# Fused attention and MLP block: weight casts behind the kept sum in ten groups, and six single operations in other places

## The chip, the cores and the metric

The kernel runs on one core of a Trainium2 chip. The metric is device time in microseconds (us), the median of several runs. Engines are named as the profile names them: PE (matrix products; PEld its weight loads), ACT (ScalarE), DVE (VectorE), POOL (GpSimd) and SP (SyncE, which issues most DMAs). Each engine works through its own instructions strictly in the order in which the program wrote them; engines wait for one another through semaphores.

## The reference

```python
x = A_x                                   # (1, 2048, 576), float32
xn = layernorm(x)
# A: sliding, dilated attention, 32 heads of 18, window 8, dilation 2
q, k, v = split(xn @ wqkv)
A = softmax(mask(q . k[pos - 2 w]) * 18**-0.5) . v[pos - 2 w] @ wo
# B: spatial shift, then an MLP with 4608 hidden columns
y  = layernorm(xn)
h  = gelu(y @ w1); hs = shift(h) @ w2     # four quarters shifted by +1, -1, +2, -2 rows
x1 = xn + hs
B  = x1 + gelu(layernorm(x1) @ w3) @ w4
out = x + A + B
```

All arithmetic is float32. The kernel makes each float32 operand into a rounded high part and a low part (the rest) and multiplies high by high, high by low and low by high; so most operands are split by a cast on ACT (the high part) and a subtraction on DVE (the low part).

## The kernel before

The 2048 rows are 16 tiles of 128 rows, or 4 blocks of 512. The program is written out in one order by hand; the Python functions only record instructions, and the place of a call in the text is the instruction's place on its engine.

*First tiles.* For each row tile: statistics (`stats_x`, DVE, with one power on POOL), normalisation in place (`norm_x`, DVE), transposes on PE (`turn_x`, `turn_tail`), and `cast_x`, which splits the transposed tile: a cast on ACT (line 311) and a subtraction on DVE (line 312). `split_tail` does the same for weights, its subtraction here on POOL (line 260). `q_part` are the products for q, k and v. Then come the shift mixer and the second layer norm.

*The MLP, first part.* Six pairs of hidden tiles run plainly, as units (c, b) of a pair c and a block b. `up(u, c, b, i)` makes one hidden tile with 14 products (line 1136) in the order of the list `PAIRS`, which takes for each row chunk k: high by high, high by low, low by high. `x1n[b]` is the normalised block; planes 0 to 4 are high parts, 5 to 8 low parts, and `split_n` writes them piece by piece on ACT (917) and DVE (900). `down` then multiplies the hidden tile with w4 into an output tile (line 1172, 12 products).

*The MLP, groups.* The other 12 pairs run as 24 groups q, twelve for each half of the rows, each with seven products of sums of blocks instead of eight plain ones. A group has 15 steps: P1 to P7 (`product`, seven matmuls each, line 1436) and D0 to D7 (`down`, twelve matmuls each, line 1172, of the group before). Their order stands in the strings `ORDER` and `ORDERS`; from group 13 on it is P1 D0 P2 P6 D1 P5 D2 P7 D3 P4 D4 P3 D5 D6 D7. What other engines do is hung on steps by `at(step, function)` and is recorded right behind the step. The pieces that matter here:

- P1 begins the sum `ca` in a PSUM bank; ACT copies it into the bank of P2 (line 1641). P6 and P7 add to `ca`, and after each of them `keep` copies the sum to SBUF on ACT (line 1442); P4 adds to the same bank once more and so must wait until the copy behind P7 has read it. `z_add` (DVE, 1446) adds another product to a kept sum, and `gelu_z` (ACT, 1124 and 1125) makes the hidden tile of it.
- `split_a(n, steps)` makes the next group's weights `w3a`: steps 0 and 1 are two casts on ACT (lines 1274 and 1276) and a small accumulating DMA from POOL (1287); step 2 is a subtraction on DVE (1280). `combine` builds sums of weights on DVE (1269), and `split_s` makes `w3s` of these in the same three steps (1274, 1276 with the DMA of line 1296, 1280).
- A step D writes one of two PSUM tiles in turn (`ps0`, `ps1`). The result leaves through ACT into a staging tile and an accumulating DMA issued by POOL (1177 and 1178; the tile must be free, that is, an earlier DMA must have landed), through ACT (1180) or through DVE (1183). Some tiles are seeded: ACT copies the old sum into PSUM ahead of the step (1153). Two steps later the tile is used again, so a late departure holds that step.

`bg` hands out the attention's work on DVE in small pieces between the steps of groups up to 18. At group 12 the half changes, and operands are split anew (`split_op`).

*The end.* The last eight down tiles run after the groups, in the loop over `j`, while `split_x` splits the attention's output blocks (ACT lines 149, 150, 155; DVE lines 151, 156); its parts are 2 (the tail chunk), 3 (chunks 0 and 1) and 1 (chunks 2 and 3), and part 0 is 2 and 3 together. The products with wo follow (line 183) and the rows are stored.

Of the kernel before, what the change touches and what calls it, by code (L numbers as in the profile page):

```python
# [37 lines left out]
NWP = NF // 2 - NPL  # L38
# [3 lines left out]
PAIRS = []  # L42
# [15 lines left out]
def fused_block(ctx, tc, x, wqkv, wo, w1, w2, w3, w4, out):  # L58
# [86 lines left out]
    def split_x(xt, part=None, scr=None):  # L145
        raw = xt.bitcast(F32)
        if part in (None, 0, 2):
            r = xt[:, 9, :] if scr is None else scr.bitcast(F32R)
            act.copy(r[64:128], raw[64:128, 4, :])
            act.copy(xt[0:64, 4, :], raw[0:64, 4, :])  # L150
            dve.tensor_tensor(xt[64:128, 4, :], raw[64:128, 4, :], r[64:128].bitcast(F32),
                              op=ALU.subtract)
        for h in {None: (0, 1), 0: (0,), 1: (1,), 2: (), 3: (0,)}[part]:
            hi, lo = slice(2 * h, 2 * h + 2), slice(2 * h + 5, 2 * h + 7)
            act.copy(xt[:, hi, :], raw[:, lo, :])
            dve.tensor_tensor(xt[:, lo, :], raw[:, lo, :], raw[:, hi, :], op=ALU.subtract)
# [55 lines left out]
    def stats_x(t):  # L212
        stats(Y[:, t, :], 0, t)
# [36 lines left out]
    def hi_main(raw, b, o, k):  # L250
        act.copy(WB[b][:, o + k, 3:5, :], raw[:, k, 1:3, :])

    def lo_main(raw, b, o, k, eng=dve):
        eng.tensor_tensor(WB[b][:, o + k, 1:3, :], raw[:, k, 1:3, :],
                          WB[b][:, o + k, 3:5, :].bitcast(F32), op=ALU.subtract)
# [72 lines left out]
    def plain_x(t):  # L328
        return x_ops(("q", t // 4)), 2 * (t % 4)
# [7 lines left out]
    def cast_x(t, tail=False):  # L337
        (cast_tail if tail else cast_main)(*plain_x(t), 2, turns[t])
# [41 lines left out]
    def spill(stg, t, c0, n):  # L380
# [5 lines left out]
                   key=lambda s: (s[1] == 0, s[1] < 3, s[2] < 3))  # L386
# [57 lines left out]
    cast_x(0)  # L444
    hi_main(r0, 0, 0, 1)
    lo_main(r0, 0, 0, 1, pool)
    stats_x(2)
    cast_x(1)
    tails(1, act.copy)
    split_tail(r0, 0, 0, pool)  # L450
    pq = {t: psa.tile([128, 512], F32, name="p1", tag="a") for t in range(2)}
# [207 lines left out]
    for p in range(3, 8):  # L659
        n = p + 1  # L660
        plan = {k: () for k in range(23)}

        def at(k, f, *args):
            plan[k] += ((f,) + args,)
# [263 lines left out]
    for t in range(NT):  # L928
# [19 lines left out]
        if t in (4, 5):  # L948
            r0, c0, n = ((256, 128, 128), (HF + 256, 0, 256))[t - 4]
# [149 lines left out]
    def temp(t, n=512):  # L1099
        return Y[:, t, :n]  # L1100
# [31 lines left out]
    def up(u, c, b, i):  # L1132
        f = c * C + i
        ps = psa.tile([128, 512], F32, name="p1", tag="a")
        for n, (a, w) in enumerate(PAIRS):
            pe.matmul(ps, W3[f][:, w, :], x1n[b][:, a, :], start=n == 0, stop=n == len(PAIRS) - 1)  # L1136
        g = temp((7, 5)[i])
        h = hid[u, i] = gelu_ps((("c12", "c22"), ("c21", "c11"))[u % 2][i], ps, g)
        low_part(h, g)
# [321 lines left out]
    otile, xo = {}, {}  # L1461
# [29 lines left out]
    def o_turn(t):  # L1491
# [4 lines left out]
    ORDER = "P1 D0 P2 P6 D1 P5 D2 P7 D3 P4 D4 P3 D5 D6 D7"  # L1496
    ORDERS = {0: "P1 P2 D0 P6 P5 P7 D1 D2 P4 P3 D3",
              NWP - 1: "P1 D0 P2 P6 P5 P7 D1 P4 P3 D2 D3 D4 D5 D6 D7",
              NWP: "D0 D1 P1 D2 P2 P6 D3 P5 P7 D4 P4 P3 D5 D6 D7"}
    spent[0] = 0.0  # L1500
    for q in range(NQ):
        sb = q // NWP
# [29 lines left out]
        n = q + 1  # L1532
# [5 lines left out]
        if q == 0:  # L1538
            at("D0", split_op, 0, "T4")
            at("P6", split_op, 0, "B22")  # L1540
            at("P7", split_a, n, (0, 1))
            at("D1", gelu22)
            at("D1", split_a, n, (2,))
            at("D1", combine, n, 0, 2)
            at("D2", combine, n, 2, 4)
            at("P3", split_s, n, (0,))
            at("P3", gelu12)
            at("P3", low22)
            at("D3", low12)
            at("D3", split_s, n, (1, 2))  # L1550
            at("D3", load_pair, q + 2)
        elif q == NWP - 1:
            rtemps[:] = [2, 13]
            at("P1", load_w4, p, 1)
            for it, k in zip(("P1", "P2", "P6", "P5", "P7", "P4", "P3"),
                             ("B11", "B21", "T2", "T1", "T3", "T4", "B22")):
                at(it, get_op, 1, k)
            at("P4", split_w4, p)
            at("P3", split_op, 1, "B11", 0)
            at("D2", split_op, 1, "B11", 1)  # L1560
            at("D3", gelu22)
            at("D4", low22)
            at("D4", split_op, 1, "B21", 0)
            at("D5", gelu12)
            at("D5", split_op, 1, "B21", 1)
            at("D6", low12)
            at("D6", split_op, 1, "T2", 0)
            at("D7", split_op, 1, "T2", 1)
        elif q == NWP:
            rtemps[:] = [2]  # L1570
            at("D0", split_op, 1, "T1", 0)
            at("D1", split_op, 1, "T1", 1)
            at("P1", split_op, 1, "T3", 0)
            at("D2", split_op, 1, "T3", 1)
            at("P2", split_op, 1, "T4", 0)
            at("P6", split_op, 1, "T4", 1)
            at("D3", split_op, 1, "B22", 0)
            at("P5", split_op, 1, "B22", 1)
            at("P5", split_a, n, (0, 1))
            at("P7", split_a, n, (2,))  # L1580
            at("P7", combine, n, 0, 2)
            at("D4", combine, n, 2, 4)
            at("D4", gelu22)
            at("P4", low22)
            at("D5", gelu12)
            at("D5", split_s, n, (0,))
            at("D6", low12)
            at("D6", split_s, n, (1, 2))
            at("D7", load_pair, q + 2)
        elif z < -1:  # L1590
            at("P1", load_w4, p, 1)
            at("P5" if q < NWP else "D2", split_a, n, (0, 1))
            at("D2" if q < NWP else "P7", split_a, n, (2,))
            at("D3", combine, n)
            at("P4", gelu22)
            at("D4", split_w4, p, 0)
            at("D4", low22)
            at("D5", split_w4, p, 1)
            at("P3", split_s, n, (0, 1))
            at("D5", gelu12)  # L1600
            at("D5", split_s, n, (2,))
            at("D6", low12)
            if z < -2:
                at("D6", load_pair, q + 2 + (q == NWP - 2))
        else:
            at("D3", split_w4, p)
            at("P4", gelu22)
            at("D4", low22)
            at("D5", gelu12)
            at("D6", low12)  # L1610
            for k, it in enumerate(("P4", "D4", "P3", "P3", "D7")):
                at(it, split_wo, k)
# [89 lines left out]
    for j in range(8):  # L1702
        tiles[j]()
        if j == 0:
            low_part(h21, Z4)
            load_y((1, 2, 3, 5))
            EV[0] = (9, 11, 10, 15, 13)
        if j in (0, 2):
            split_x(xo[0], j // 2)
        if j == 6:  # L1710
            split_x(xo[1], 0)
        if j == 2:
            read_xo(2, xp_tile(3))
        if j == 5:
            load_y((7,))
            read_xo(3, ring_block(("o", 3)))
# [4 lines left out]
    for t in range(NT):  # L1721
        b, i = divmod(t, 4)
# [55 lines left out]
```

## Time and profile before

| what | us |
|---|---|
| median of 3 runs | 1268.59 (1267.49 to 1269.87) |
| the profiled execution, its own time | 1268.14 |
| its span from first to last instruction | 1266.4 |
| PE busy | 1254.4 |
| DVE busy | 933.0 |
| ACT busy | 761.6 |

The profile lists instructions with their start and duration in us from the span's start; in brackets stands how long the engine was idle just before, and what ended that. Rows with xN are N instructions of one kind in a row. Matmuls overlap a little: a step's modelled duration is longer than the distance from its start to the next step's start, so times lost on PE are read from distances between starts.

### The profile page before, as it was taken

To read this page: it belongs to the slowest core of one execution; us is meant where nothing else is said; L and a number is where in the kernel's file an instruction comes from. 1 tells how busy PE (TensorE), PEld (TensorE's weight loads), DVE (VectorE), ACT (ScalarE), POOL (GpSimd) and SP (SyncE) were. 2 spreads that over 40 slices of the span, in tenths; PEclk is the share of its full clock that TensorE was granted. 3 is DMA by queue.
4 is the path that set the end of the run, shared out by engine and by line. 5 is a ranking of instruction groups with operands and counts; after the bars stand their busy time and mean duration, and the time that the engine had idled before them with its cause. 6 is when DMAs were issued, how large, how long until landed. Compare 5 with 4: busy or idle time off the path is not lost.

```text
span 1266.4 us, 20999 instructions
## 1 busy us (share of the span) xinstructions
PE 1254.4 (99%) x7819; PEld 1156.8 (91%) x7819; DVE 933.0 (74%) x1207; ACT 761.6 (60%) x1271; POOL 266.9 (21%) x408
## 2 busy tenths in 40 slices
PE   8999999999999999999999999999999999999998
PEld 8999998899898999999889999998888899899998
DVE  7877646688558999997759998989889884464441
ACT  4455457526645545455867767776677776677620
POOL 2213200011222211212222232222122222222200
PEclk9999999999999999999999999999999999999999
DMA  7638994447888986769679898888968769899972
GB/s 220 157 85 199 229 197 146 149 130 198 200 230 180 222 158 147 159 135 245 124 175 192 194 200 190 189 166 206 249 111 183 141 116 194 185 213 223 263 245 84
DMA packets 208654, 228.92 MB, mean 181 GB/s; under 512 B 80920, under 2 KB 142328, under 8 KB 208424
## 3 DMA queue, kind: packets, MB, share of 16 engines
q1 hardware_dynamic: 175800, 160.79, 45.2%
q0 software_dynamic: 32752, 66.80, 32.6%
q8 instruction: 61, 1.00, 0.3%
q14 instruction: 41, 0.34, 0.1%
HBM read 127.71 MB, written 110.23 MB: 188 GB/s over the span
## 4 chain that ended last, share of the span: by engine, by line
PE 42%; issue 5%; DMA 2%; POOL 1%; ACT 1%; DVE 0%; POOLq 0%; ACTq 0%
PE ps L1172 20%; PE cc L1436 18%; PE ps L183 4%; DMA yd<-Y 1%; POOL yd L1178 1%; DMA w3s<-w3st 1%; PE p L1745 0%; DVE w3st L1269 0%; ACT Y L1177 0%; POOL w3s L1296 0%; ACT xt L1240 0%; ACT w3s L1274 0%; ACT cc L1641 0%; ACT Y L1442 0%; POOL w3a L1287 0%
## 5 line engine op out<-in xcount | busy, mean ns | idle before, releaser
L1172 PEld LDWEIGHTS ps<-w,c 128*128 128x128 f32 x3456 | 478.2, 189 | 15.3 <-ACT Y L1177 1.4
L1172 PE MATMUL ps<-w,c 128*128 128x288 f32 x3456 | 487.7, 296 | 1.1 <-ACT Y L1177 0.6
L1178 POOL DMA_DIRECT2D yd<-Y x154 | 138.0, 899 | 391.9 <-ACT Y L1177 333.0
L1130 DVE TENSOR_TENSOR c<-Y,c 128x512 fp32r<-128x512 f32 x144 | 98.8, 688 | 91.5 <-ACT Y L1119 87.9
L1177 ACT COPY Y<-ps 128x576 f32<-128x576 f32 x154 | 97.8, 636 | 80.5 <-PE ps L1172 68.3
L1436 PE MATMUL cc<-xt,w3s 128*128 128x512 f32 (+1 forms) x504 | 128.1, 393 | 0.9 <-DMA w3s<-w3st 0.9
L1436 PEld LDWEIGHTS cc<-xt,w3s 128*128 128x128 f32 (+1 forms) x504 | 92.4, 188 | 19.5 <-DMA w3s<-w3st 1.7
L1180 ACT COPY Y<-ps 128x576 f32<-128x576 f32 x89 | 56.9, 640 | 64.8 <-PE ps L1172 63.1
L1436 PE MATMUL cc<-x1n,w3a 128*128 128x512 f32 (+1 forms) x336 | 85.4, 393 | 0.9 <-ACT cc L1641 0.9
L1050 DVE TENSOR_TENSOR po<-q,k 128x1152 f32<-128x1152 f32 (+1 forms) x48 | 84.2, 1755 | 0.8
L1053 DVE TENSOR_REDUCE L<-po 128x64 f32<-128x1152 f32 (+1 forms) x48 | 84.0, 1751 | 0.8
L1118 ACT ACTIVATE c<-p 128x512 fp32r<-128x512 f32 x48 | 28.7, 597 | 84.8 <-PE p L1136 84.8
L1446 DVE TENSOR_TENSOR Y<-cc,Y 128x512 f32<-128x512 f32 x49 | 33.7, 688 | 59.4 <-ACT Y L1442 54.5
L1026 DVE TENSOR_TENSOR po<-v,L 128x1152 f32<-128x1152 f32 x56 | 75.4, 1354 | 0.9
L393 PE MATMUL p<-wb,xt 128*128 128x288 f32 (+1 forms) x504 | 71.8, 300 | 1.5 <-ACT stg L398 0.9
L1436 PEld LDWEIGHTS cc<-x1n,w3a 128*128 128x128 f32 (+1 forms) x336 | 60.5, 188 | 11.8 <-ACT cc L1641 1.2
L393 PEld LDWEIGHTS p<-wb,xt 128*128 128x128 f32 (+1 forms) x504 | 67.8, 189 | 3.4 <-ACT stg L398 1.3
L1030 DVE TENSOR_TENSOR po<-po 128x1152 f32<-128x1152 f32 x49 | 66.4, 1355 | 0.9
L600 PE MATMUL ca<-wb,xt 128*128 128x288 f32 x420 | 61.5, 297 | 0.4 <-DVE keep L611 0.4
L1153 ACT COPY ps<-Y 128x576 f32<-128x576 f32 x89 | 57.5, 646 | 3.1 <-DVE Y L1183 1.2
L113 POOL TENSOR_TENSOR rs<-rs,mhalf 128x1 f32<-128x1 f32 x32 | 18.8, 587 | 190.0 <-DVE mv L116 109.8
L600 PEld LDWEIGHTS ca<-wb,xt 128*128 128x128 f32 x420 | 57.6, 189 | 0.9 <-DVE keep L611 0.6
(256 smaller groups left out, 2150.8 us busy)
## 6 DMA issues: line engine op xcount, KB each, us to landing
yd<-Y POOLq DMA_DIRECT2D x156, 288.0 KB, 6.0
Y<-in_B_w_dram SPq DMA_DIRECT2D x29, 576.0 KB, 5.6
w3st<-in_B_w_dram SPq DMA_DIRECT2D x56, 256.0 KB, 8.1
qkvd<-stg SPq DMA_DIRECT2D x66, 144.0 KB, 3.3
yd<-ev POOLq DMA_DIRECT2D x26, 288.0 KB, 6.5
w3st<-in_B_w_dram SPq DMA_DIRECT2D x92, 64.0 KB, 7.7
xd<-st SPq DMA_DIRECT2D x16, 320.0 KB, 4.9
xd<-big SPq DMA_DIRECT2D x16, 320.0 KB, 6.7
```

Source lines behind the costliest of these rows:

```text
L393: pe.matmul(ps[:, :QB], xo[:n, o + k, a, :], W[:n, w + k, v, :], start=i == 0, stop=i == len(PLAIN) - 1)
L600: pe.matmul(ps[:, :QB], xo[:n, XO[x], a, :], W[:n, OP[w], v, :], start=start and i == 0, stop=stop and i == len(HALVES) - 1, skip_group_ch ...
L1026: dve.tensor_tensor(dst, vv, Lf[:, :, w:w + 1].to_broadcast([128, TPP * GH, HD]), op=ALU.mult)
L1030: dve.tensor_tensor(o, o, dst, op=ALU.add)
L1050: dve.tensor_tensor(dst, qf[:, None, :].to_broadcast([128, n, TPP * GC]), win, op=ALU.mult)
L1053: dve.tensor_reduce(Lw[:, w:w + n, :], dst.rearrange("p w (x d) -> p w x d", d=HD), axis=AX.X, op=ALU.add)
L1130: dve.tensor_tensor(h[:, 1, :], g, h[:, 0, :].bitcast(F32), op=ALU.subtract)
L1153: act.copy(ps[:, :, :HF], halves(t))
L1172: pe.matmul(ps[:, k, :HF], h[:, col], w[:, p, k * HF:(k + 1) * HF], start=n == 0 and not seed, stop=n == len(seq) - 1, skip_group_check=True)
L1177: act.copy(e.rearrange("p (h c) -> p h c", h=2), ps[:, :, :HF])
L1178: pool.dma_start(yd[t], e, accum_op=ALU.add)
L1436: pe.matmul(ps, WX[w][:k, v, SLOT[w], :], area[sb][xk][:k, a, :], start=onto is None and i == 0, stop=last and i == len(HALVES) - 1, skip_ ...
```

## The change

One thing is done in ten groups (13 to 22), and six single operations change place elsewhere. No instruction is added, removed or resized.

```diff
     lo_main(r0, 0, 0, 1, pool)
+    cast_x(1)
     stats_x(2)
-    cast_x(1)
     tails(1, act.copy)
...
     def up(u, c, b, i):
...
-        for n, (a, w) in enumerate(PAIRS):
+        pairs = PAIRS
+        if (u, i) == (2, 0):
+            pairs = sorted(PAIRS, key=lambda s: (s[0] in (5, 6, 7, 8), s[0] % 5 in (2, 3)))
+        for n, (a, w) in enumerate(pairs):
...
-              NWP: "D0 D1 P1 D2 P2 P6 D3 P5 P7 D4 P4 P3 D5 D6 D7"}
+              NWP: "D0 P1 D1 D2 P2 P6 D3 P5 P7 D4 P4 P3 D5 D6 D7"}
...
         if q == 0:
-            at("P3", split_s, n, (0,))
+            at("P3", split_s, n, (0, 1))
             at("P3", gelu12)
             at("P3", low22)
             at("D3", low12)
-            at("D3", split_s, n, (1, 2))
+            at("D3", split_s, n, (2,))
...
         elif q == NWP:
             at("P4", low22)
+            at("P3", split_s, n, (0, 1))
             at("D5", gelu12)
-            at("D5", split_s, n, (0,))
+            at("D5", split_s, n, (2,))
             at("D6", low12)
-            at("D6", split_s, n, (1, 2))
...
         elif z < -1:
-            at("P5" if q < NWP else "D2", split_a, n, (0, 1))
-            at("D2" if q < NWP else "P7", split_a, n, (2,))
+            at("P5" if q < NWP else "P7", split_a, n, (0, 1))
+            at("D2" if q < NWP else "D3", split_a, n, (2,))
             at("D3", combine, n)
...
-        if j in (0, 2):
-            split_x(xo[0], j // 2)
+        if j in (0, 1, 3):
+            split_x(xo[0], {0: 2, 1: 3, 3: 1}[j])
```

Here `NWP` is 12, `q` the group and `z` is q - 24. Since three lines are added ahead, lines after 1136 have numbers higher by 3 in the changed kernel.

The ten groups, on ACT in group 13 around step P7, before (`ps_9478` is the tile of D2, `ps_9540` that of D4, `ps_9516` that of D3, `cc_9450` the bank of the sum):

```order
L1180 COPY Y<-ps_9478 128x576
L1153 COPY ps_9540<-Y 128x2x288
L1274 CAST w3a<-w3st 128x768
L1276 ACTIVATE w3a<-w3st,kv 96x384
L1442 COPY Y<-cc_9450 128x512
L1177 COPY Y<-ps_9516 128x576
L1124 ACTIVATE c_9584<-Y 128x512
```

And the same place in the changed kernel:

```order
L1183 COPY Y<-ps_9478 128x576
L1156 COPY ps_9540<-Y 128x2x288
L1445 COPY Y<-cc_9450 128x512
L1277 CAST w3a<-w3st 128x768
L1279 ACTIVATE w3a<-w3st,kv 96x384
L1180 COPY Y<-ps_9516 128x576
L1124 ACTIVATE c_9584<-Y 128x512
```

The two casts moved from ahead of the copy of the kept sum to behind it, still ahead of D3's departure.

Group 12, on ACT from the end of P4 to the seed of the next group's D0, before (`c_9361` and `c_9395` are hidden tiles, `ps_9314`, `ps_9358` and `ps_9394` the tiles of D5, D6 and D7, `ps_9421` that of the next D0):

```order
L1125 ACTIVATE Y<-Y 128x512
L1177 COPY Y<-ps_9314 128x576
L1124 ACTIVATE c_9395<-Y 128x512
L1125 ACTIVATE Y<-Y 128x512
L1274 CAST w3s<-w3st 128x1024
L1177 COPY Y<-ps_9358 128x576
L1153 COPY ps_9421<-Y 128x2x288
L1276 ACTIVATE w3s<-w3st,kv 96x512
L1177 COPY Y<-ps_9394 128x576
```

And in the changed kernel:

```order
L1125 ACTIVATE Y<-Y 128x512
L1277 CAST w3s<-w3st 128x1024
L1279 ACTIVATE w3s<-w3st,kv 96x512
L1180 COPY Y<-ps_9314 128x576
L1124 ACTIVATE c_9399<-Y 128x512
L1125 ACTIVATE Y<-Y 128x512
L1180 COPY Y<-ps_9358 128x576
L1156 COPY ps_9418<-Y 128x2x288
L1180 COPY Y<-ps_9398 128x576
```

Both casts of w3s now stand ahead of D5's departure and of the gelu.

The end, on ACT behind the tail chunk's casts, before (`ps_12057` is the tile of j = 1, `ps_12101` that of j = 3):

```order
L150 CAST x1n_11886<-x1n_11886 64x512
L155 CAST x1n_11886<-x1n_11886 128x1024
L1177 COPY Y<-ps_12057 128x576
L155 CAST x1n_11886<-x1n_11886 128x1024
L1177 COPY Y<-ps_12101 128x576
```

And in the changed kernel, where `ps_12099` is j = 3:

```order
L150 CAST x1n_11886<-x1n_11886 64x512
L1180 COPY Y<-ps_12057 128x576
L155 CAST x1n_11886<-x1n_11886 128x1024
L1180 COPY Y<-ps_12099 128x576
L155 CAST x1n_11886<-x1n_11886 128x1024
```

Each of the two big casts moved behind a departure. On DVE nothing moved there: the subtraction of line 156 that needs the first cast still stands ahead of the departure of the tile of j = 2.

## The prediction

> **What bounds the kernel now.** I read the busy times first, then the chain that ended last, then every idle stretch of PE and of its weight loads, and then ACT, DVE and POOL around each.
>
> ```profile
> PE 1254.4 (99%) x7819; PEld 1156.8 (91%) x7819; DVE 933.0 (74%) x1207; ACT 761.6 (60%) x1271; POOL 266.9 (21%) x408
> 639.64 1.60 PE ps L1172 x12
> 641.24 1.61 PE cc L1436 x7
> ```
>
> PE is busy 99% of the span, and the chain of waits (the last two rows here are from it) runs along PE: a D step takes 1.60 us, a P step 1.61. The change leaves the number of matmuls alone, so it can only win or lose the places where PE stands still. A group of seven P and eight D steps should take 7 x 1.61 + 8 x 1.60 = 24.07 us. In the second half it takes more:
>
> ```profile
> 936.43 1.89 PE L1436 MATMUL cc<-xt,w3a 128*128 128x512 f32 x7 [0.28 <-ACT Y L1442]
> ...
> 960.80 1.46 PEld L1436 LDWEIGHTS cc<-xt,w3a 128*128 128x128 f32 x7 [0.23 <-ACT Y L1442]
> 985.17 1.47 PEld L1436 LDWEIGHTS cc<-xt,w3a 128*128 128x128 f32 x7 [0.23 <-ACT Y L1442]
> ```
>
> These are P4 of groups 13, 14 and 15, each waiting for the kept sum of P7. From 960.80 to 985.17 are 24.37 us, 0.30 more than the steps need; the ten groups 13 to 22 show the same wait.
>
> **The change, part by part.**
>
> *The ten groups.* ACT around P7 of group 15, with the later casts and D5 to D7:
>
> ```profile
> 981.80 1.78 PE L1436 MATMUL cc<-x1n,w3s 128*128 128x512 f32 x7
> 982.73 0.64 ACT L1153 COPY ps<-Y 128x576 f32<-128x576 f32 x1
> 983.30 0.83 ACT L1274 CAST w3a<-w3st 128x768 fp32r<-128x768 f32 x1
> 984.04 0.61 ACT L1276 ACTIVATE w3a<-w3st,kv 96x384 fp32r<-96x384 f32 x1
> 984.56 0.56 ACT L1442 COPY Y<-cc 128x512 f32<-128x512 f32 x1
> 986.74 2.34 DVE L1269 TENSOR_TENSOR w3st<-w3st 128x384 f32<-128x384 f32 x4
> 990.32 1.05 ACT L1274 CAST w3s<-w3st 128x1024 fp32r<-128x1024 f32 x1
> 991.92 0.64 ACT L1177 COPY Y<-ps 128x576 f32<-128x576 f32 x1
> 990.12 4.96 PE L1172 MATMUL ps<-w,c 128*128 128x288 f32 x36
> ```
>
> P7 ends at 983.58, but the copy starts at 984.56, behind two casts, and ends at 985.12; P4 starts at 985.17. With the casts behind it the copy starts at about 983.61 and ends at 984.17. P4 could start 0.30 earlier, at 984.87, so the wait goes whole: 10 x 0.30 = 3.0 us won. The casts then run from about 984.1 to 985.4, some 0.2 later than before, and D3's departure by as much; D3's tile is next wanted by D5 at 990.12, so the DMA issue and the departure are covered by more than 4 us. On DVE the subtraction for w3a moves behind D3's step and up to one or two attention pieces, but the added product ahead of it starts about 0.95 earlier, so the combined weights (ready at 989.08 here) come at most about 1 us later, and ACT takes the w3s cast only at 990.32. D7 needs D5's tile at 990.12 + 3.2 - 0.3 = 993.02, and its departure ends at 992.56: 0.46 us of cover. I cost the moved casts at nothing; without that cover each group would lose what exceeds 0.46.
>
> *The hidden tile of unit 2.*
>
> ```profile
> 328.49 0.73 PE L1136 MATMUL p<-x1n,w3a 128*128 128x512 f32 x2
> 329.75 6.19 PE L1136 MATMUL p<-x1n,w3a 128*128 128x512 f32 x26 [0.53 <-DVE x1n L900]
> 335.77 4.42 PE L1172 MATMUL ps<-w,c 128*128 128x288 f32 x32
> 330.28 0.68 DVE L900 SCALAR_TENSOR_TENSOR x1n<-x1n 128x512 fp32r<-128x512 f32 x1
> ```
>
> Two hidden tiles are 28 products of 0.23 (1.61 / 7), 6.44 us, and took 7.28: the third product waits for a low plane. In the new order ten products on high planes come first, 2.3 us, until 330.8; the last low plane is ready at 330.96 and wanted by the fourteenth product at 331.5. All 0.84 goes, and nothing else is late: I take -0.8.
>
> *Group 0.* The tail cast of w3s moves from behind the gelu to right behind the main cast.
>
> ```profile
> 634.05 1.54 PE L1436 MATMUL cc<-xt,w3s 128*128 128x512 f32 x6
> 635.92 0.50 PE L1436 MATMUL cc<-xt,w3s 96*128 96x512 f32 x1 [0.33 <-DMA w3s<-w3st]
> 630.60 0.73 ACT L1276 ACTIVATE w3s<-w3st,kv 96x512 fp32r<-96x512 f32 x1
> 631.81 4.07 DMA w3s<-w3st
> ```
>
> The seventh product of P6 should start at 634.05 + 6 x 0.23 = 635.43 and waits until 635.92 for the DMA that starts 1.2 after the cast. The cast goes about 1.6 earlier (a gelu of two ACT instructions and a departure stood between), so the DMA lands near 634.2: -0.5. The gelu slips by 0.7; I see no step that wants it sooner.
>
> *Group 12: P1 ahead of D1, and the casts of w3s ahead of the gelu.*
>
> ```profile
> 899.78 1.76 PE L1172 MATMUL ps<-w,c 128*128 128x288 f32 x12
> 902.47 1.89 PE L1436 MATMUL cc<-x1n,w3a 128*128 128x512 f32 x7 [0.93 <-ACT cc L1641]
> 900.77 0.64 ACT L1177 COPY Y<-ps 128x576 f32<-128x576 f32 x1 [2.99 <-DMA yd<-Y]
> 917.26 0.64 ACT L1177 COPY Y<-ps 128x576 f32<-128x576 f32 x1 [2.29 <-PE ps L1172]
> 922.15 1.63 PEld L1172 LDWEIGHTS ps<-w,c 128*128 128x128 f32 x12 [0.54 <-ACT ps L1153]
> 925.54 1.56 PE L1436 MATMUL cc<-xt,w3s 128*128 128x512 f32 x6
> 927.63 0.50 PE L1436 MATMUL cc<-xt,w3s 96*128 96x512 f32 x1 [0.53 <-DMA w3s<-w3st]
> ```
>
> Before, ACT sits 2.99 us in D1's departure, for a staging tile, and the copy that P2 needs stands behind it. P2 could start at 899.78 + 1.60 = 901.38 and starts at 902.47. With P1 one step earlier its copy stands ahead of that departure: -1.1. D3, which wants D1's tile, comes two steps after P2, when the departure is over. Behind the group, D0 of group 13 stands 0.54 by its weight loads for its seed, and P6 waits from 925.54 + 6 x 0.23 = 926.92 to 927.63 for the DMA of w3s. With both casts of w3s earlier the seed loses one cast from its front (-0.4) and the DMA starts some 4 us earlier (-0.7). Against it: the casts need the combined weights. PE would reach D5 about 1.1 earlier, at 914.3, and end it at 916.0; but by DVE's queue the combining ends at about 915.7, so the casts (1.05 and 0.73 like those above, 1.6 one behind the other) hold ACT until 917.3. D5's departure ends near 918.0, and D7, which wants its tile at 914.3 + 3.2 = 917.5, waits about 0.6: a new stall. Bounds: nothing, if DVE gains the 1 us too, and 1.6, if the casts are wholly late; I take +0.6. Group 12 sums to -1.1 - 0.4 - 0.7 + 0.6 = -1.6.
>
> *The first tiles.* The subtraction of tile 1 goes ahead of tile 2's statistics on DVE.
>
> ```profile
> 11.67 0.41 PE L304 MATMUL ps<-ident,stg 128*128 128x128 f32 x2 [0.72 <-DVE xt L312]
> 11.63 1.43 POOL L260 TENSOR_TENSOR wb<-rawa,wb 32x576 fp32r<-32x576 f32 x1
> 6.43 0.57 DVE L120 TENSOR_SCALAR Y<-Y,mv,rs 128x576 f32<-128x576 f32 x1
> 12.01 1.37 DVE L120 TENSOR_SCALAR Y<-Y,mv,rs 128x576 f32<-128x576 f32 x1
> 15.09 1.06 PE L393 MATMUL p<-wb,xt 128*128 128x288 f32 x6 [0.45 <-ACT stg L398]
> ```
>
> The wait of 0.72 at 11.67 goes. But the statistics, POOL's power and the weights' subtraction of line 260 behind it all slip by about 0.66 (the subtraction of 512 columns at 330.28 takes 0.68), and PE's next products need both that subtraction, which would end at 13.7 instead of 13.06, and the normalised tile 2. So PE saves 0.7 and meets the next wait. It can win at most the 0.45 at 15.09, and lose the slip of 0.66; I take 0, halfway. The row at 12.01 took 1.37 where the same instruction took 0.57 at 6.43, while POOL's ran. The Trainium skill (SBUF — State Buffer, "Who interferes with whom") says that such a DVE instruction and POOL share one pair of ports, which the one that starts first keeps until it is done; the trace agrees, and by that rule DVE, now first by some 0.05 us, would delay POOL instead, for a term of about +0.1.
>
> *The end.* A big cast of ACT moves behind the departure of j = 1.
>
> ```profile
> 1195.17 8.27 PE L1172 MATMUL ps<-w,c 128*128 128x288 f32 x60 [0.60 <-ACT Y L1177]
> 1194.48 0.64 ACT L1177 COPY Y<-ps 128x576 f32<-128x576 f32 x1 [0.23 <-DMA yd<-Y]
> 1194.28 1.23 DVE L156 TENSOR_TENSOR x1n<-x1n 128x1024 fp32r<-128x1024 f32 x1 [0.48 <-ACT x1n L155]
> 1195.43 0.75 DVE L1183 TENSOR_TENSOR Y<-ps,Y 128x576 f32<-128x576 f32 x1
> ```
>
> PE waits at j = 3 for j = 1's departure. But that one waited for a DMA, not for the cast, so it can't start sooner: nothing won. The cast now runs from 1195.0 to 1196.1, the subtraction of line 156 to 1197.3, and the departure of j = 2 behind it (1195.43 here) to 1198.0. j = 4 wants that tile at 1195.17 + 1.60 = 1196.8: +1.2 lost. Bounds: +0.1, if the DMA lands over 1 us sooner so that PE wins its wait, and +1.4.
>
> The sum is -3.0 - 0.8 - 0.5 - 1.6 + 0 + 1.2 = -4.7 us on the profiled execution's 1268.14, or 1263.4. That execution lies 0.45 under the median of the runs, so I forecast 1263.7 between the two.
>
> **The rivals.**
>
> 1. *The two new stalls don't come* (D7 of group 12, j = 4). For it: both rest on queues that I carried forward by hand over ten and four instructions. Against: each has its order written down. The time is 1263.7 - 0.6 - 1.1 = 1262.0.
>
> 2. *The wait of the ten groups moves to D7.* Late combining on DVE, or a w3a cast that waits for its load, would push the w3s cast and D5's departure. For it: only 0.46 us of cover. Against: ACT has slack ahead of the w3s cast in every group, and DVE idles before the added product. If the push is 0.76, each group loses the 0.30 again: 1263.7 + 3.0 = 1266.7, about as before.
>
> 3. *The same place, worse: slower.* If an attention piece and a late load push the departure by 1.9, each group waits 1.4 at D7: 1263.7 + 14 = 1277.7. It decides from a push of 1.2 (0.46 of cover and (4.7 + 2.5) / 10 = 0.72 lost in each group), which is a full 1.35 us attention product beyond what I counted. From group 19 on there is no attention, which speaks against it.
>
> **How the numbers follow.** About 0.2% (2.5 us) is what a measurement of this kernel can tell from no change. Forecast 0.62 (by itself 1262.3 to 1265.2), rival 1 0.18, rival 2 0.14, rival 3 0.06. Faster by over 0.2% are the first two and a quarter of rival 2: 0.83; within 0.2% the rest of rival 2: 0.11; slower 0.06. The range for 8 in 10 reaches to rival 1 with the start's best end (-0.4) and the group 12 bound, 1261.2, and up to rival 2, 1266.7.
>
> **What would show it.** In the changed trace: P4 of groups 13 to 22 without an idle row, and 24.1 us from one P4 to the next; no idle in unit 2's hidden tile; P6 of groups 0 and 13 not waiting for a DMA; P2 of group 12 right behind D2; a new wait before D7 of group 12 on ACT and at j = 4 on DVE line 1186 (1183 before). I am wrong if the period of the second half stays at 24.4, or if D7 waits in every group; the size is wrong if the end costs nothing or the start gains.

## The result, and the profile after

The changed kernel took 1265.33 us (median, 1263.91 to 1268.49), the kernel before 1268.41 us (1266.48 to 1269.87) on the same chip: a ratio of 0.9978 with a 95% interval of 0.9972 to 0.9985, or 2.8 us faster (1.9 to 3.6); the two medians lie 3.1 apart. The forecast was 1263.7 in a range of 1261.2 to 1266.7. The sign, the range and the main mechanism held; the sum of -4.7 did not.

The profiled execution of the changed kernel took 1263.99 us with a span of 1262.2, at the low end of its runs. Against the profiled execution of before (span 1266.4) that is -4.2, more than the medians give. The last paragraph on the prediction, on the sum, says where the rest comes from.

Busy times, from the page of the changed kernel: PE has 4.2 us less, the other engines the same work.

```profile
PE 1250.2 (99%) x7819; PEld 1156.1 (92%) x7819; DVE 934.4 (74%) x1207; ACT 760.9 (60%) x1271; POOL 267.4 (21%) x408
```

*The ten groups.* First P4 of groups 13, 14 and 15 on PE, then ACT around P7 of group 15 (start and duration in us, engine, line, operation; line numbers are 3 higher than before):

```profile
933.35 1.78 PE L1439 MATMUL cc<-xt,w3a 128*128 128x512 f32 x7
957.44 1.78 PE L1439 MATMUL cc<-xt,w3a 128*128 128x512 f32 x7
981.54 1.78 PE L1439 MATMUL cc<-xt,w3a 128*128 128x512 f32 x7
...
980.14 0.59 ACT L1445 COPY Y<-cc 128x512 f32<-128x512 f32 x1 [0.24 <-PE cc L1439]
980.62 0.84 ACT L1277 CAST w3a<-w3st 128x768 fp32r<-128x768 f32 x1
981.36 0.62 ACT L1279 ACTIVATE w3a<-w3st,kv 96x384 fp32r<-96x384 f32 x1
```

The copy of the kept sum now stands ahead of the two casts, and no P4 of these groups has an idle time ahead of it. The period is 24.10 (957.44 to 981.54) where it was 24.37.

*Unit 2, group 0 and group 12* on PE, and ACT around the new waits:

```profile
328.65 6.54 PE L1139 MATMUL p<-x1n,w3a 128*128 128x512 f32 x28
335.02 4.95 PE L1175 MATMUL ps<-w,c 128*128 128x288 f32 x36
340.36 1.87 PE L1175 MATMUL ps<-w,c 128*128 128x288 f32 x12 [0.39 <-ACT Y L1180]
...
633.94 1.77 PE L1439 MATMUL cc<-xt,w3s 128*128 128x512 f32 x7
...
900.66 1.78 PE L1439 MATMUL cc<-x1n,w3a 128*128 128x512 f32 x7
913.54 3.36 PE L1175 MATMUL ps<-w,c 128*128 128x288 f32 x24
917.18 1.87 PE L1175 MATMUL ps<-w,c 128*128 128x288 f32 x12 [0.28 <-ACT Y L1180]
926.92 1.78 PE L1439 MATMUL cc<-xt,w3s 128*128 128x512 f32 x7
```

```profile
337.56 0.63 ACT L909 ACTIVATE Y<-x1n 64x512 fp32r<-64x512 f32 x1 [1.24 <-DMA x1n<-xn]
...
338.75 1.04 ACT L913 ACTIVATE x1n<-x1n 128x1024 fp32r<-128x1024 f32 x1
339.69 0.62 ACT L1180 COPY Y<-ps 128x576 f32<-128x576 f32 x1
...
914.93 1.06 ACT L1277 CAST w3s<-w3st 128x1024 fp32r<-128x1024 f32 x1 [2.53 <-DVE w3st L1272]
915.89 0.72 ACT L1279 ACTIVATE w3s<-w3st,kv 96x512 fp32r<-96x512 f32 x1
916.51 0.62 ACT L1180 COPY Y<-ps 128x576 f32<-128x576 f32 x1
```

The wait inside the hidden tile of unit 2 (328.65) is gone, but the unit's last D step waits instead (340.36), for a departure on ACT that stands behind the split of the next block of rows (lines 909, 910 and 913), whose loads landed only at 337.56. P6 at 633.94 and P6 of group 13 (926.92) run as one row of seven: no wait for a DMA. (The first is P6 of group 1, whose w3s group 0 makes; the prediction speaks of it under group 0.) P2 of group 12 (900.66) waits for nothing, and D7 (917.18) has the new wait for D5's departure, behind the casts of w3s.

*The first tiles and the end:*

```profile
13.24 0.65 PE L300 MATMUL ps<-ident,Y 128*128 128x128 f32 x4 [1.22 <-DVE Y L120]
11.43 1.76 DVE L120 TENSOR_SCALAR Y<-Y,mv,rs 128x576 f32<-128x576 f32 x1 [0.21 <-POOL rs L113]
11.47 1.40 POOL L260 TENSOR_TENSOR wb<-rawa,wb 32x576 fp32r<-32x576 f32 x1
...
1189.74 1.86 PE L1175 MATMUL ps<-w,c 128*128 128x288 f32 x12 [0.87 <-ACT Y L1180]
1192.62 6.66 PE L1175 MATMUL ps<-w,c 128*128 128x288 f32 x48 [1.01 <-DVE Y L1186]
```

The wait of 0.72 for the subtraction is gone, and PE stands 1.22 for the normalisation of tile 2 instead, which took 1.76. At the end PE waits twice, at j = 3 as before and, new, at j = 4 for DVE line 1186. The idle times in brackets are a little short, since a step's modelled end is late; by the distances between starts PE loses 1.03 at j = 3 and 1.28 at j = 4.

The same stretches in five traces, each from the start of one step of PE to the start of another, in us. "Start" runs from DVE's first statistics (so that the landing of the first tile is out of it) to the products of line 600 that begin at 100.15 in the kernel before; unit 2 from its predecessor's last D steps (322.06 before) to its successor's first (348.53); group 0 from its P1 to D1 of group 1; group 12 from P4 of group 11 to P7 of group 13; the ten groups from there to P4 of group 23; the end from there to the first product of line 183.

| stretch | before | ten groups alone | six moves alone | changed | all mended |
|---|---|---|---|---|---|
| start | 96.04 | 95.59 | 96.57 | 96.32 | 95.87 |
| unit 2 | 26.47 | 25.76 | 26.13 | 26.18 | 25.52 |
| group 0 | 24.73 | 24.81 | 24.14 | 24.13 | 24.13 |
| group 12 | 50.76 | 50.13 | 48.84 | 48.83 | 48.41 |
| ten groups | 247.20 | 244.15 | 246.90 | 244.14 | 244.15 |
| end | 23.30 | 23.44 | 24.68 | 24.84 | 22.43 |

The columns with a part of the change undone are experiments, which follow.

### The profile page after: what moved, and what is told of

It reads as the page before. It is cut to its first block, busy times and chain, and to the rows that moved or that the text cites. A ratio compares the mean times of both kernels' runs of the same rounds, so it can differ in the third digit from the quotient of the medians.

```text
span 1262.2 us, 21012 instructions
## 1 busy us (share of the span) xinstructions
PE 1250.2 (99%) x7819; PEld 1156.1 (92%) x7819; DVE 934.4 (74%) x1207; ACT 760.9 (60%) x1271; POOL 267.4 (21%) x408
## 4 chain that ended last, share of the span: by engine, by line
PE 66%; issue 2%; DMA 2%; ACT 1%; DVE 1%; POOL 0%; SPq 0%; POOLq 0%; ACTq 0%
PE ps L1175 32%; PE cc L1439 20%; PE p L1139 10%; PE ps L183 4%; DMA v<-qkvd 1%; DMA yd<-Y 1%; DMA xt<-td1T 0%; PE p L1748 0%; POOL yd L1181 0%; DVE Y L1186 0%; DVE w3st L1272 0%; DVE xt L900 0%; ACT Y L1119 0%; ACT Y L1180 0%; ACT x1n L155 0%
```

## The experiments

My theory after the two traces: the ten groups give their whole 3.0, and the six single moves together another 1.2, as the two traces have it. The rival, which the medians favoured: the six are worth next to nothing, since the end (+1.5), the start and unit 2 take back what groups 0 and 12 win. Each run below was timed beside runs of the kernel before; the ratios are to those. An interval of such a ratio is 2.3 to 3.4 us wide, so what a single move is worth is read from its stretch in the traces, and the total only has to be compatible.

### The ten groups alone

The kernel before, with two lines of the change:

```diff
-            at("P5" if q < NWP else "D2", split_a, n, (0, 1))
-            at("D2" if q < NWP else "P7", split_a, n, (2,))
+            at("P5" if q < NWP else "P7", split_a, n, (0, 1))
+            at("D2" if q < NWP else "D3", split_a, n, (2,))
```

> The kernel before with the change in the ten groups 13 to 22 alone. My theory (each group loses exactly the wait of the kept sum and nothing else): P4 of the ten groups without an idle row, 24.1 us from one P4 to the next, no idle row at D7; 10 x 0.30 = 3.0 us faster than before, and its trace agrees with that of before up to group 12 within 0.2 us. Rival (the gain of the groups is partly handed back behind them): the same period of 24.1, but the span shorter by less than 2.4, with a longer wait in the last eight D steps.

1264.84 us against 1267.75 (0.9972, 0.9960 to 0.9983). P4 of groups 13 to 15 in its trace:

```profile
933.53 1.78 PE L1436 MATMUL cc<-xt,w3a 128*128 128x512 f32 x7
957.62 1.78 PE L1436 MATMUL cc<-xt,w3a 128*128 128x512 f32 x7
981.71 1.78 PE L1436 MATMUL cc<-xt,w3a 128*128 128x512 f32 x7
```

The stretch of the ten groups is 3.05 shorter (247.20 to 244.15), the end is not longer (23.44 against 23.30): nothing is handed back. But "its trace agrees with that of before up to group 12 within 0.2 us" failed. With the same program up to there, this trace is 1.0 us ahead at the start, 0.7 in unit 2, and its P2 of group 12 waits 0.29 where before waited 0.93. These are differences between executions, not between kernels, and they are as large as the terms of my sum.

### The six single moves alone

The changed kernel with those two lines put back.

> The changed kernel with the ten groups put back to the old order, so that only the six single moves are left. My theory, from the ledger of the two traces (start -0.2, unit 2 +0.1, group 0 -0.6, group 12 and the start of 13 about -2, end +1.5): 1.2 us faster than before. The sum as I had forecast it would be 1.7 us faster. Rival (by the medians of the runs the whole change is worth 3.1, not the 4.2 of the two traces): 0.1 us faster, within what can be told from nothing.

1267.30 us against 1267.75 (0.9998, 0.9989 to 1.0007): the rival. The moves that win (group 0, group 12) and those that lose (start, end) cancel within what can be told. The table has each: against the run of the ten groups alone, start +1.0, group 0 -0.7, group 12 -1.3, end +1.2.

### The start put back

```diff
-    cast_x(1)
     stats_x(2)
+    cast_x(1)
     tails(1, act.copy)
```

> The changed kernel with the first tiles' order put back (statistics of tile 2 ahead of the subtraction of tile 1). My forecast put this move at 0, and the two traces at -0.2. New theory, from four more traces: the move costs about 0.7, since the turn of tile 2 now waits 1.2 for its normalisation where the old order waited 0.5 to 0.7 for the subtraction; the trace of the kernel before hides it, since its first tile landed 0.5 later and its statistics of tile 2 waited 0.33 for a DMA. It expects, from the first statistics to the first step behind 99 us, 95.6 instead of 96.3 to 96.6, no wait over 0.5 before the turn of tile 2, and 0.7 us faster than the changed kernel. Rival (the move is neutral, and the differences are the landing of the first loads): 96.3 again, and the same time.

1263.31 us (0.9962, 0.9950 to 0.9975) where the changed kernel stands at 0.9978. From the first statistics to the same products it took 95.88, in spite of 0.18 in which tile 2 was not there yet; the eight traces with the new order and this subtraction on POOL have 96.32 to 96.95, mean 96.58, the five with the old order 95.59 to 96.04, mean 95.81. So the move at the start costs 0.8 on average. The PE and DVE rows of the old order in this run:

```profile
10.94 0.41 PE L304 MATMUL ps<-ident,stg 128*128 128x128 f32 x2 [0.73 <-DVE xt L312]
...
11.28 1.36 DVE L120 TENSOR_SCALAR Y<-Y,mv,rs 128x576 f32<-128x576 f32 x1
```

The normalisation of tile 2 starts at 11.28 here and ends at 12.64; in the changed kernel, whose first tile landed within 0.06 of this one, it ends at 13.19. These 0.55 are the whole cost in four of the eight traces (96.32 to 96.39). In the other four DVE also stands idle ahead of the moved subtraction (line 312), here in the kernel with the end's cast one step later:

```profile
9.42 0.69 DVE L312 TENSOR_TENSOR xt<-ps,xt 128x512 fp32r<-128x512 f32 x1 [0.60 <-ACT xt L311]
```

It waits 0.20 to 0.61 for the cast of line 311, which in two of these traces stands on ACT behind a cast of weights (line 251) that waited 0.33 and 0.41 for its load, and start is longer by as much (96.57 to 96.95). In the old order the statistics of tile 2 stood ahead of that wait.

### The subtraction of line 260 on DVE

```diff
-    split_tail(r0, 0, 0, pool)
+    split_tail(r0, 0, 0)
```

> The changed kernel with the weights' subtraction of line 260 on DVE instead of POOL, where it stands ahead of the normalisation of tile 2. My theory (the normalisation takes 1.76 instead of 0.57 because POOL's subtraction runs beside it): the normalisation takes 0.57, the subtraction some 0.7 on DVE, the wait before the turn of tile 2 falls from 1.2 to about 0.6 and the kernel is 0.5 to 0.6 us faster than the changed one. Rival (the normalisation is slow for another reason, its operand from POOL for one): it takes 1.76 again and ends 0.7 later, and the kernel is 0.5 us slower.

1264.24 us (0.9968, 0.9955 to 0.9980). DVE and POOL in its trace:

```profile
11.25 0.75 DVE L260 TENSOR_TENSOR wb<-rawa,wb 32x576 fp32r<-32x576 f32 x1
12.48 0.58 DVE L120 TENSOR_SCALAR Y<-Y,mv,rs 128x576 f32<-128x576 f32 x1
...
11.30 1.11 POOL L113 TENSOR_TENSOR rs<-rs,mhalf 128x1 f32<-128x1 f32 x1 [0.93 <-DVE rs L112]
```

The normalisation takes 0.58 instead of 1.76: it is the POOL subtraction beside it that stretches it. The wait before the turn of tile 2 falls from 1.22 to 0.58, and start takes 96.06, 0.5 less than the mean of the new order. POOL's power of line 113, which takes 0.55 elsewhere, now takes 1.11 beside DVE's subtraction: here POOL is the slower one.

### Unit 2: the departure ahead of the big cast

```diff
             if (u, i) == (2, 1):
-                split_n(u + 1, x1n[u + 1], 0, RT)
+                split_n(u + 1, x1n[u + 1], 2, RT)
...
             if (u, j) == (2, 1):
+                split_n(3, x1n[3], 3, RT)
                 split_n(3, x1n[3], 1, RT)
```

> The changed kernel with the second unit's big split of the next tokens (line 913) behind the departure of j = 1 instead of ahead of it. My theory (what the hidden tile of unit 2 wins is lost at the last down step of the unit, whose bank waits for that departure, which stands behind casts that wait for the landing of the next tokens): the departure starts about 338.75 instead of 339.69, the wait of 0.39 at 340.36 goes, and PE is 0.5 us earlier from there on, to the end; 0.5 us faster than the changed kernel. Rival (the next hidden tile wants those planes and waits instead): the wait comes back inside the hidden tile at 342, and the time is the same.

1265.19 us (0.9972, 0.9960 to 0.9983): no gain to be told. PE's weight loads in its trace, then ACT:

```profile
339.77 1.63 PEld L1175 LDWEIGHTS ps<-w,c 128*128 128x128 f32 x12 [0.28 <-ACT Y L1180]
341.35 0.32 PEld L1139 LDWEIGHTS p<-x1n,w3a 128*128 128x128 f32 x2
341.99 5.77 PEld L1139 LDWEIGHTS p<-x1n,w3a 128*128 128x128 f32 x26 [0.33 <-DVE x1n L900]
...
337.91 0.63 ACT L909 ACTIVATE Y<-x1n 64x512 fp32r<-64x512 f32 x1 [1.85 <-DMA x1n<-xn]
```

The wait at the last D step shrinks, but part of it comes back as the third product of the next hidden tile, and both hang on the same landing (337.91): that of the next block of rows, which lines 895 and 897 load and whose last part line 909 waits for. Unit 2 takes 26.01 here. Without this edit nine traces with the new order of products have 25.9 to 26.4 and once 27.0 (there line 909 starts at 338.60), the two with the old order 26.47 and 25.76. In all eleven the next unit's D steps start 10.87 to 10.93 after line 909 does. So what unit 2 takes is set by when these loads land, 6.7 to 7.9 us after the issue of line 895, and not by the order of the products. With this edit the distance is 10.12: at an equal landing it is worth 0.76. The total does not show that, since the landing came late in this trace, 15.89 after the start of the unit where ten of the eleven have 14.9 to 15.5.

The trace shows a wait at P4 of group 4, too:

```profile
715.78 1.89 PE L1440 MATMUL cc<-xt,w3a 128*128 128x512 f32 x7 [0.17 <-ACT Y L1446]
...
712.66 0.84 ACT L1277 CAST w3a<-w3st 128x768 fp32r<-128x768 f32 x1 [2.81 <-DMA w3st<-in_B_w_dram]
```

Here, in the first half, the kept sum still stands behind the casts, and the casts wait for a late load. Some other traces have this wait as well, whether or not they come early.

### Group 12: the casts behind D5's departure

```diff
-            at("P3", split_s, n, (0, 1))
+            at("D5", split_s, n, (0, 1))
             at("D5", gelu12)
-            at("D5", split_s, n, (2,))
             at("D6", low12)
+            at("D6", split_s, n, (2,))
```

> The changed kernel with the two casts of w3s in group 12 behind the departure of D5 instead of ahead of it (still ahead of the gelu). My theory (the casts wait 2.5 for the combining and hold D5's departure, for which D7 waits): the wait of 0.28 (0.51 by the weight loads) before D7 goes, PE reaches D0 of group 13 about 0.45 earlier, and P6 of group 13 still waits for no DMA; 0.4 us faster than the changed kernel. Rival (the casts, now 1.6 later, bring back the seed's wait at D0 of group 13 or the DMA's at P6): one of those waits of 0.5 is back, and the time is the same.

1264.12 us (0.9970, 0.9958 to 0.9982). PE from D5 to D0 of group 13:

```profile
913.73 4.96 PE L1175 MATMUL ps<-w,c 128*128 128x288 f32 x36
918.52 1.78 PE L1439 MATMUL cc<-x1n,w3a 128*128 128x512 f32 x7
920.18 1.86 PE L1175 MATMUL ps<-w,c 128*128 128x288 f32 x12
921.88 1.78 PE L1439 MATMUL cc<-x1n,w3a 128*128 128x512 f32 x7
```

D5, D6 and D7 run as one row of 36, and neither the seed nor P6 makes PE wait longer than 0.1. The stretch of group 12 is 48.42 against 48.83 in the changed kernel: the stall at D7 cost 0.41. In one other trace with the changed order of these casts PE loses 0.8 there.

### Group 12: P1 behind D1 again

```diff
-              NWP: "D0 P1 D1 D2 P2 P6 D3 P5 P7 D4 P4 P3 D5 D6 D7"}
+              NWP: "D0 D1 P1 D2 P2 P6 D3 P5 P7 D4 P4 P3 D5 D6 D7"}
```

> The changed kernel with P1 of group 12 behind D1 again. My theory (the copy that P2 needs stands behind D1's departure, which waits for the transfer out of a staging tile): an idle row before P2 of group 12 on ACT L1641, of 0.3 to 0.9 as in the kernel before and in the run of the ten groups alone, since the end of that transfer is not tied to PE; 0.3 to 1.1 us slower than the changed kernel from there on. Rival (the gain of the move was the landing of that transfer by chance): no idle row there, the same time.

1265.75 us (0.9980, 0.9970 to 0.9990).

```profile
901.32 1.89 PE L1439 MATMUL cc<-x1n,w3a 128*128 128x512 f32 x7 [0.22 <-ACT cc L1644]
918.60 1.87 PE L1175 MATMUL ps<-w,c 128*128 128x288 f32 x12 [0.92 <-ACT Y L1180]
...
916.35 1.05 ACT L1277 CAST w3s<-w3st 128x1024 fp32r<-128x1024 f32 x1 [2.52 <-DVE w3st L1272]
```

Group 12 takes 49.98, 1.15 more than with the move; the total does not tell it (0.9980 against 0.9978). By the distances between starts 0.50 of it stands at P2, where I had put all of it (ACT waited 2.29 for the staging tile here, 2.99 in the kernel before). The other 0.64 stands at D7: without the move the gelu behind P2 is later too, DVE's queue with it, and the w3s cast starts 1.42 later than in the changed kernel's trace while D5 starts only 0.78 later.

### The end: old order, one step later, and other staging tiles

The three edits, one for each kernel, in the order of the results below:

```diff
-        if j in (0, 1, 3):
-            split_x(xo[0], {0: 2, 1: 3, 3: 1}[j])
+        if j in (0, 2):
+            split_x(xo[0], j // 2)
```

```diff
-        if j in (0, 1, 3):
-            split_x(xo[0], {0: 2, 1: 3, 3: 1}[j])
+        if j in (0, 2, 3):
+            split_x(xo[0], {0: 2, 2: 3, 3: 1}[j])
```

```diff
-            EV[0] = (9, 11, 10, 15, 13)
+            EV[0] = (10, 15, 13, 9, 11)
```

> The changed kernel with the end's casts where they were (both halves of the first split behind j = 0, the rest behind j = 2). My theory (the move at the end is the dearest part of the change): the wait at j = 4 on DVE goes, the wait at j = 3 on the staging tile's DMA is as before (0.6 to 0.9), and the last D steps take 1.2 to 1.5 less than in the changed kernel; 1.3 us faster than the changed kernel. Rival (the older order meets the same DMA in another place and the end costs 1.5 in both): the same time.

1263.58 us (0.9959, 0.9947 to 0.9972). The end takes 23.37 as before, with the one wait of 0.67 at j = 3. So the move at the end costs 1.5. (Seven traces with the moved casts have 24.65 to 25.56, three with the old order 23.29 to 23.44.)

> The changed kernel with the big cast of the end moved once more, from behind j = 1 to behind j = 2. My theory (the subtraction of that cast on DVE stands ahead of the departure of j = 2 and makes PE wait at j = 4): the wait of 1.01 at j = 4 goes, the one of 0.87 at j = 3 stays; 1.1 us faster than the changed kernel. Rival (something else sets when L183 may start, the loads of Y for one): the wait moves to a later j or to the first L183, and the time is as that of the changed kernel.

1263.87 us (0.9966, 0.9953 to 0.9978). The wait at j = 4 goes, but half of it comes back two steps on:

```profile
1190.29 5.07 PE L1175 MATMUL ps<-w,c 128*128 128x288 f32 x36 [0.69 <-ACT Y L1180]
1195.80 3.46 PE L1175 MATMUL ps<-w,c 128*128 128x288 f32 x24 [0.45 <-DVE Y L1186]
...
1193.85 1.23 DVE L156 TENSOR_TENSOR x1n<-x1n 128x1024 fp32r<-128x1024 f32 x1 [1.42 <-ACT x1n L155]
1195.00 0.75 DVE L1186 TENSOR_TENSOR Y<-ps,Y 128x576 f32<-128x576 f32 x1
```

The second big cast, behind j = 3, does to j = 4's departure what the first had done to j = 2's. The end takes 24.09: 0.75 won of the 1.1 expected.

> The changed kernel with the five staging tiles of the end in another order, so that the departure of j = 1 takes one that no transfer has used (15) instead of 11. My theory (that departure waits for a DMA and not for the cast): it starts at about 1187.6 instead of 1189.05, PE has no wait at j = 3 (-1.0), and as the big cast stands behind it, that is earlier too and the subtraction ends in time, so that the wait at j = 4 goes as well: 2.0 us faster than the changed kernel. Rival (the DMA queue is full there, and the later departures wait for their tiles instead): the waits move to j = 5 and j = 7 and the gain is under 0.5.

1263.18 us (0.9962, 0.9950 to 0.9975).

The departure of j = 1 in the changed kernel, then in this one the same departure and cast on ACT and the D steps on PE:

```profile
1189.05 0.64 ACT L1180 COPY Y<-ps 128x576 f32<-128x576 f32 x1 [1.45 <-DMA yd<-Y]
...
1187.33 0.63 ACT L1180 COPY Y<-ps 128x576 f32<-128x576 f32 x1
1187.86 1.05 ACT L155 CAST x1n<-x1n 128x1024 fp32r<-128x1024 f32 x1
...
1190.89 6.67 PE L1175 MATMUL ps<-w,c 128*128 128x288 f32 x48 [0.59 <-DVE Y L1186]
```

With a free staging tile j = 1's departure starts at 1187.33 and waits for nothing, and the wait at j = 3 is gone: that departure had waited for a transfer, not for the cast. The wait at j = 4 falls to 0.59 but does not go. The end takes 23.28, 1.56 less than in the changed kernel.

### All places mended

The changed kernel with the start as before, the edits of unit 2 and of group 12, the other staging tiles, the two big casts of the end behind j = 2 and j = 4, and the order of the ten groups in group 3 too:

```diff
-        if j in (0, 1, 3):
-            split_x(xo[0], {0: 2, 1: 3, 3: 1}[j])
+        if j in (0, 2, 4):
+            split_x(xo[0], {0: 2, 2: 3, 4: 1}[j])
...
-            at("P5" if q < NWP else "P7", split_a, n, (0, 1))
-            at("D2" if q < NWP else "D3", split_a, n, (2,))
+            at("P5" if q < NWP and q != 3 else "P7", split_a, n, (0, 1))
+            at("D2" if q < NWP and q != 3 else "D3", split_a, n, (2,))
```

> The changed kernel with each place mended where a run showed a loss: the first tiles as before; unit 2's big split behind the departure; the w3s casts of group 12 behind D5's departure; the end's staging tiles in the other order, its two big casts behind j = 2 and j = 4; and the casts of w3a behind the kept sum in group 3 too, the one group of the first half where a late load made P4 wait in some traces. If the places add up: start -0.7, unit 2 and group 3 -0.4, group 12 -0.45, end -2.1 for the staging tiles and -0.6 for j = 4, in all 4.2 under the changed kernel's 1265.3, 1261.1 us; no idle row of PE from 135 us to the output product. Rival (the cover is used up and new stalls take half of it): 1263 us.

1260.71 us against 1268.32 (0.9936, 0.9924 to 0.9949): 4.6 under the changed kernel's median, 5.3 by the two ratios, where 4.2 were expected; its interval lies wholly below that kernel's, so it beats both. PE's D steps of the end, and a P4 of the first half:

```profile
1182.81 13.49 PE L1175 MATMUL ps<-w,c 128*128 128x288 f32 x100
1196.14 4.03 PE L183 MATMUL ps<-Wo,x1n 128*128 128x288 f32 x29
...
763.39 1.89 PE L1440 MATMUL cc<-xt,w3a 128*128 128x512 f32 x7 [0.20 <-ACT Y L1446]
```

The end has no wait left (22.43). But I had counted the groups of the first half wrongly: group 3 is not among those that wait, and P4 of groups 4, 6 and 7 lost 1.1 in all to late loads. The last run puts the casts behind the kept sum in all of them (`"P7"` and `"D3"` without a condition).

> The kernel with all places mended (best2), and the casts of w3a behind the kept sum in every group of the first half, not in group 3 alone. In best2 that edit stood in a group that did not wait: its trace loses 0.3, 0.4 to 0.5 and 0.4 at P4 of the groups near 715, 763 and 788 us, where the kept sum stands behind casts that wait up to 2.4 for their load. My theory (it is the order of those casts, as in the second half, and PE being earlier than before uncovers it): these three waits go, 24.1 from one P4 to the next through the first half too, 1.1 us faster than best2, about 1259.6 us. Rival (the load itself is late, and with the casts behind the kept sum the wait moves to D3's departure, the combining and D7): the waits turn up at D5 or D7 of the same groups and the time is that of best2.

1260.17 us against 1268.10 (0.9935, 0.9921 to 0.9948). The waits at P4 are gone, none came at D5 or D7, and the first half takes 245.81 from D1 of group 1 to P4 of group 11 where the kernel with all places mended took 246.90. The total is only 0.5 under that kernel's, and the ratios are alike (0.9935 and 0.9936). In this trace the loads of unit 2 landed late again (338.14), which took 0.55 beforehand. So the groups come later here, and the changed kernel, which comes as late, takes 245.76 for the same stretch without the edit. Only in group 4 did the loads land as late here as where P4 waited (line 1264's last at 713.8, with P7 at 712.44; in the run of unit 2 alone at 713.3 and 712.23, where P4 lost 0.33), and here P4 did not wait. That the order of the casts takes away such a wait is shown in that one group; what the move is worth in all or on average is not.

## Why the prediction was right or wrong

*The ten groups: right.* "10 x 0.30 = 3.0" measured 3.06 in the traces and a ratio of 0.9972 alone, and the moved casts cost nothing, at D7 or elsewhere: all twelve traces with the new order have 244.14 or 244.15. Rivals 2 and 3, which rested on the 0.46 us of cover, did not happen in any trace.

*Group 0: right.* -0.5 forecast, 0.6 to 0.7 measured. No run puts this move back alone; twelve traces with it have 24.13 or 24.14 for the stretch, the two without 24.73 and 24.81.

*Group 12: right in sum, in part for another reason.* -1.6 forecast; -1.9 between the two traces, -1.3 against the run in which before's order had a shorter wait. The new stall at D7 came (+0.6 forecast, 0.41 measured), so rival 1 failed there. But "P2 could start at 901.38 and starts at 902.47 ... -1.1" took one execution's wait for the whole price. The staging transfer ends when it ends: by the distances between starts P2 lost 1.1 in the trace of before and 0.4 and 0.5 in two other traces with the old order. The move kept its worth because it also brings DVE's queue forward, which I had only as a bound ("nothing, if DVE gains the 1 us too").

*Unit 2: wrong.* The step that failed is "All 0.84 goes, and nothing else is late". The traces show no gain from the order (25.9 to 27.0 against 25.8 and 26.5). The bound stood in the trace of before and I did not read on to it, the departure of j = 1 on ACT:

```profile
339.74 0.62 ACT L1177 COPY Y<-ps 128x576 f32<-128x576 f32 x1
```

It stands behind the split of the next block of rows and ends at 340.36; the last D step, which waits for it, starts at 335.77 + 3 x 1.60 = 340.57. At most 0.2 of the 0.84 could be kept. And the wait of the third product was itself in part that execution's: in the other trace with the old order the two hidden tiles took 6.59, not 7.28.

*The first tiles: wrong.* "I take 0, halfway" should have been the upper end, +0.66: measured 0.8, of which 0.55 is the normalisation and the rest, in some traces, a wait for a cast that stands behind a late load. Both mechanisms were there (PE's next wait is for the normalisation, and POOL's subtraction runs beside it); the mistake was to give a saved wait of 0.7 full credit against a slip when the next product waits for the slipped instruction itself.

*The end: right.* +1.2 was forecast at j = 4, and by the distances between starts PE loses 1.28 there, in all seven traces with the moved casts. The other 0.3 of the 1.5 is at j = 3, whose wait for the staging tile did not shrink: it is 0.84 to 1.43 in these seven and 0.76 to 0.91 in the three with the old order. Whether the move made it longer is not shown.

*The sum.* With the sizes measured over all runs: ten groups -3.06, group 0 -0.65, group 12 -1.3, start +0.8, end +1.5, unit 2 nothing: -2.7, against 2.8 (1.9 to 3.6) measured. The two traces alone give -4.2, because the trace of before was late in three places that the change only seems to mend: its first tile landed 0.53 later (statistics at 4.11 against 3.58) and its third by 0.33, unit 2's third product waited, and the staging transfer of group 12 was slow. My sum was made against that execution and carried the same error. That the -4.7 lies near the -4.2 of the two traces is in part luck: of its 0.8 for unit 2 they have 0.3, and 0.5 of theirs is the landing of the first tile, which it did not count.

## What to carry to other kernels

Before a wait is counted as won, follow PE to the next instruction that waits for something outside its own chain (a landing, a staging tile): the slack there, not the wait, is what can be kept. A wait for a DMA that is read from one execution has a spread of its own; where the trace of before shows it once, forecast it as a range that reaches down to nothing. And an instruction that is moved forward on one engine's queue helps or hurts whoever stands behind it: the same edit that cleared ten groups (a copy ahead of two casts) lost 1.5 at the end, where a departure came to stand behind a subtraction.

## What the runs showed of the hardware

DVE's normalisation of 128 x 576 takes 0.57 to 0.63 where POOL's subtraction does not run beside it, 1.27 to 1.37 when it starts 0.4 to 0.5 behind POOL's subtraction of 1.4, and 1.76 when both start together (11.43 and 11.47; 0.04 apart in all eight traces). In all of these it ends 0.3 us behind POOL's. The Trainium skill (SBUF — State Buffer, "Who interferes with whom") lets whoever issues first keep the shared ports, and by that DVE, recorded 0.04 first, should have gone through undisturbed. Here it did not; a difference of 0.04 may be less than the records of the two engines tell, so the rule is not refuted, but an order so close can't be counted on. In the run with line 260 on DVE, where DVE started 0.05 first (11.25 and 11.30), it was POOL that was slowed, 0.55 to 1.11, as that section of the Trainium skill says.

From the issue of the loads of the next block of rows (lines 895 and 897) to ACT's instruction that waits for them (line 909) passed 6.7 to 7.9 us, different from execution to execution, and unit 2, which waits for them, took 25.8 to 27.0 us without its edit.
